# Expert layer's second half: pairs of token tiles prepared per unit, three wide result instructions, more units in pair form

## The chip, the cores and the metric

The kernel runs on one core of one Trainium2 chip. The metric is the device time in microseconds (us) of one execution. The engines are TensorE (PE, matrix products; PEld is its weight load), VectorE (DVE), ScalarE (ACT), GpSimd (POOL) and SyncE (SP, which issues the DMAs).

## The reference, cut to what matters

Three layers follow one another: an attention over 32 pooled memory slots, a layer `g = h * cos(h)` between two products, and a layer of four experts. The change lies in the expert layer:

```python
def _moe2_ref(x, domain_probs, w1, w2):        # x 2304x512, w1 4x512x1024, w2 4x1024x512
    p = domain_probs / (domain_probs.sum(-1, keepdims=True) + 1e-09)
    for e in range(E):
        h = np.maximum(x @ w1[e], 0.0)
        out += p[:, e:e + 1] * (h @ w2[e])
```

All products are carried at about float32 precision: a value is split into a high and a low float32r part, and each product is three matmuls (high by high, high by low, low by high; `mm3`, L340 to L349).

## The kernel before, in words

**Tiling.** The expert layer is cut into 64 units `(u, s, j)`: `u` is one of two halves of the tokens (1152 each), `s` one of 16 slices of 256 hidden features, `j` one of two groups of tokens in a half: 512 tokens (`j=0`, four tiles of 128) and 640 tokens (`j=1`, five tiles).

**First product of a unit** (`hidden`, L1233): `x @ w1` for one slice, as a 2x2 block product in Strassen-Winograd form, with seven block products instead of eight. Each has two chunks of the inner dimension and three matmuls, so a unit is 42 matmuls of 256 or 320 columns. Sums of block products are grown in a PSUM bank, with copies of intermediate states taken by ACT (`a1`, `a2`, `a3`) and sums by DVE (`c11`, `c22`, `c12`). `rectify` (L1296) applies the maximum with zero.

**Second product** (`h @ w2`, added into `acc` with the weight `p`) has two forms. In the *whole* form (`plain_out`, L1384) a tile of 128 tokens takes two feature chunks by three matmuls of 512 columns, and one DVE instruction of 512 elements takes the result out (`gather`, L1098). In the *pair* form (`pair_prep`, L1446 on, `pair_out`, L1525 on) two tiles form a 2x2 block product with seven block products of three matmuls of 256 columns. It needs sums of blocks of `h` beforehand (`sm`), split in high and low (DVE or POOL, and ACT), and prepared sums of blocks of `w2` (`wt`). Its results are taken out between the products: before the change in five instructions of 256 elements and one of 512 per pair, and in the second half of the tokens one of the five runs on ACT into a buffer `ev`, and DVE or POOL adds that to `acc` (`grown`, `plus`).

**Which unit has which form** (`mode`): in `u=0`, slices 2 to 4 are pairs in both groups, slices 5 to 12 in `j=0` alone, all else is whole: 14 of 32 units are pairs. In `u=1` all are pairs but the last. The fifth tile of a `j=1` pair unit goes in the whole form alone (`one_prep`).

**What is around it.** `build_x` makes the seven split operands of the tokens for a group: (0,1) and, at the turn between the halves, (1,0) and (1,1), on ACT, DVE and POOL, with the buffers `sA` and `sB`. `make_wa`, `make_wb` split the weights of slices 7 to 15 during `u=0`; they are stored, and fetched again for `u=1`.

**The order of the work** is fixed when the program is built: `Order` (L167 on) holds tasks that yield operations, estimates when each could start, and issues the earliest, or an older-ranked one within a patience (`PATIENCE`, `RK`). Two settings keep TensorE's operands early: `SLACK` adds a margin in ns to the estimated readiness of an operation of TensorE, by stretch of the work, and `STALL` adds 160 ns where a result would be there less than 60 ns ahead. Buffers are rings (`RINGS`), taken in turn. PSUM has eight banks: four in a ring `p`, four in a ring `po`. The plan of the layers before (`PLAN`) is written out by hand and holds up to about 375 us.

Of the kernel before, what the change touches and what calls it, by code (L numbers as in the profile page):

```python
# [9 lines left out]
F32 = mybir.dt.float32  # L10
# [55 lines left out]
class Have:  # L66
    def __init__(self, keys):
# [73 lines left out]
             p2=2, raw2=2, tt=1, wa=2, wb=2, wt=2, cq=2, p1=2, u2=2, u3=1, ht0=1, ht1=1, h7=4, h7a=2, h7f=3, h1a=1, sma=2, h1=1, sm=2, p=4, po=4, ev=4, eva=2)  # L141
HALVES = (0,)
MERGED = ()
PATIENCE = ({"PE": 0.2, "ACT": 0.5, "DVE": 0.5, "POOL": 0.5, "SP": 0.5, "X": 0.0},
# [3 lines left out]
RK = ((0, -2, 8, 13, 20), (0, -2, 8, 12, 8), (0, -2, 3, 13, 8), (0, -2, 8, 13, 20))  # L148
EV, ONE_P = ((), (0,)), True
RX = (8, 305, 337)  # L150
LAST_PAIR, BP0, WR = 13, 1.5, (-12, 0)
BW, BP, BX, RL = (20.0, 1.5), 1.5, (0.8, 0.8), -15
HOP = 90.0
STALL, SLACK = 160.0, ({"PE": 200.0}, {"PE": 200.0}, {"PE": 300.0}, {"PE": 200.0})
TURNS = (3, 9, 31)
AHEAD = (2, 3, 4, 5, 6)
FULL = (2, 3, 4)
THROUGH = (3, 31)
# [120 lines left out]
def tile_kernel(  # L279
# [13 lines left out]
    nc = tc.nc  # L293
# [511 lines left out]

    def w1_steps(raw, tt, wa):
# [19 lines left out]
    def ready(s):  # L826
# [35 lines left out]
        for f in mixes_of(tt, q[:, 0, 0], q[:, 0, 1], q[:, 1, 0], q[:, 1, 1]):  # L862
            o = yield Op("POOL", 745, lambda: f(nc.gpsimd), t1, port=("POOL",))
# [21 lines left out]
    def ahead(s):  # L885
# [35 lines left out]
        for f in mixes_of(tt, q[:, 0, 0], q[:, 0, 1], q[:, 1, 0], q[:, 1, 1]):  # L921
            o4 = yield either(416, 740, f, o, t1, free=20.0)
# [147 lines left out]
    def mode(i):  # L1070

        u, s, j = units[i]
        if u:
            return "one" if i == FINAL else "pair"
        return "pair" if s in FULL or not j and FULL[-1] < s < LAST_PAIR else "whole"

    def tiles_of(i):

        n = 2 * SUBS[units[i][2]][1] // 128
        if mode(i) == "pair":  # L1080
            return ((n - 2, n - 1), (0, 1)), list(range(2, n - 2))
        return (), list(range(n))

# [66 lines left out]
    def make_wb(s):  # L1150
# [18 lines left out]
        for f in mixes_of(tt, q[:, 0, 0], q[:, 0, 1], q[:, 1, 0], q[:, 1, 1]):  # L1169
            o4 = yield either(416, 740, f, o, t1, free=BW[s > TURNS[0] // 2])  # L1170
# [37 lines left out]
    def build_x(u, j):  # L1208
        if u:
            yield have(*((f"O{i}.{k}e", e) for i, (u_, s, _) in enumerate(units) if not u_ and s and mode(i) == "pair"  # L1210
                         for k in range(2) for e in EV[0]))
            yield have(*(("h7", i, k) for i, (u_, _, _) in enumerate(units) if not u_ and mode(i) == "pair" for k in range(2)))
# [20 lines left out]
    def hidden(i):  # L1233
# [43 lines left out]
        R[rz].give(kz, c11)  # L1277
        R["p1"].give(k1, c11)
# [11 lines left out]
        mids[i] = c, kc, px, kx, py, ky, u2, k2, a2, o4, c11, c22, last, tc_  # L1290
# [5 lines left out]
    def rectify(i):  # L1296
# [29 lines left out]
        hts[i] = which, kh
        if s > FULL[-1]:
# [386 lines left out]
```

## Time and profile before

| | us |
|---|---|
| time, median of 3 runs (lowest to highest) | 1120.25 (1119.69 to 1120.79) |
| span of the profiled execution, first to last instruction | 1118.8 |
| PE busy / weight load busy | 1109.8 / 1055.6 |
| DVE busy | 879.0 |
| POOL busy | 668.5 |
| ACT busy | 583.7 |

The span is the profiled execution's own time; the median of the timed runs is 1.45 us longer, which is what lies around the span. A product on PE lasts longer than the distance to the next one's start, since products are pipelined: how fast PE works is read from the distance between starts.

### The profile page before, as it was taken

What the parts mean: (1) busy time and instruction counts of PE and PEld (TensorE: products, weight loads), DVE (VectorE), ACT (ScalarE), POOL (GpSimd) and SP (SyncE); (2) the same over time, 40 slices, a digit from 0 to 9 for tenths busy, and PEclk for the clock granted to TensorE, in tenths of its full rate; (3) what the DMA queues carried; (4) which work ended last, traced back from release to release, by engine and by line L of the source; (5) the groups of instructions that cost most, each with busy time, mean ns of one, the idle gap of its engine ahead of it and who ended that gap; (6) DMA issues with size and microseconds to landing.
All of it is one profiled execution on the core that took longest, in us unless ns stands there. A gap on an engine that the chain in (4) does not pass through costs nothing.

```text
span 1118.8 us, 22424 instructions
## 1 busy us (share of the span) xinstructions
PE 1109.8 (99%) x8698; PEld 1055.6 (94%) x8698; DVE 879.0 (79%) x1619; ACT 583.7 (52%) x1219; POOL 668.5 (60%) x1001
## 2 busy tenths in 40 slices
PE   9899999999999999999999999999999999999998
PEld 8689999999999989999999999989999999999997
DVE  5888988898888765777888888778777777777776
ACT  4887766565655424444444543445455545554543
POOL 1455556665677404665767664217587877777774
PEclk9999999999999999999999999999999999999999
DMA  9940636167614037443566456683554345434532
GB/s 305 359 137 25 213 129 228 57 227 266 254 39 180 1 118 250 161 161 114 186 253 237 181 181 232 247 337 130 191 205 174 142 167 214 185 142 154 215 131 86
DMA packets 44299, 201.76 MB, mean 180 GB/s; under 512 B 6176, under 2 KB 15392, under 8 KB 29984
## 3 DMA queue, kind: packets, MB, share of 16 engines
q1 hardware_dynamic: 44192, 200.33, 49.1%
q8 instruction: 68, 1.11, 0.4%
q14 instruction: 39, 0.32, 0.1%
HBM read 132.68 MB, written 67.63 MB: 179 GB/s over the span
## 4 chain that ended last, share of the span: by engine, by line
PE 97%; DMA 1%; DVE 1%; SPq 0%; ACT 0%; issue 0%
PE op L342 52%; PE hp L342 41%; DMA q<-in_qt_dram 1%; PE vw_ps L629 1%; PE warm L765 1%; PE kvp L513 1%; PE spare L757 1%; PE sc L566 0%; SPq L370 0%; PE pe L487 0%; DVE st L576 0%; PE pkt L535 0%; DVE sA L390 0%; ACT u L373 0%; DVE stT L596 0%
## 5 line engine op out<-in xcount | busy, mean ns | idle before, releaser
L342 PE MATMUL hp<-x,wa 128*128 128x320 f32 (+1 forms) x2688 | 405.7, 296 | 0.7 <-ACT u L373 0.5
L1103 DVE SCALAR_TENSOR_TENSOR acc<-op,p_all,acc 128x256 f32<-128x256 f32 (+1 forms) x566 | 301.9, 566 | 121.6 <-PE op L342 117.3
L342 PEld LDWEIGHTS hp<-x,wa 128*128 128x128 f32 x2688 | 373.6, 188 | 5.7 <-ACT u L373 1.2
L342 PE MATMUL op<-gt,wo 128*128 128x288 f32 x1536 | 218.1, 296 | 0.0
L342 PEld LDWEIGHTS op<-gt,wo 128*128 128x128 f32 x1536 | 208.1, 188 | 4.5 <-issue 2.4
L390 POOL TENSOR_TENSOR sm<-c 128x128 f32<-128x128 f32 x180 | 88.2, 496 | 157.6 <-ACT c L373 156.5
L342 PE MATMUL op<-wb,h 128*128 128x256 f32 (+1 forms) x786 | 144.7, 298 | 0.0
L342 PE MATMUL op<-wt,h 128*128 128x256 f32 x888 | 143.3, 281 | 0.0
L373 ACT ACTIVATE u<-hp 128x320 f32<-128x320 f32 (+1 forms) x128 | 52.6, 411 | 154.3 <-PE hp L342 154.3
L342 PEld LDWEIGHTS op<-wt,h 128*128 128x128 f32 x888 | 124.7, 189 | 2.4
L342 PEld LDWEIGHTS op<-wb,h 128*128 128x128 f32 x786 | 116.8, 189 | 3.9
L342 PE MATMUL op<-wb,hg 128*128 128x512 f32 (+1 forms) x477 | 115.5, 385 | 0.0
L342 PE MATMUL hp<-attnT,vw 128*128 128x288 f32 x768 | 113.2, 296 | 0.2 <-DVE attnT L390 0.2
L342 PEld LDWEIGHTS hp<-attnT,vw 128*128 128x128 f32 x768 | 105.2, 188 | 3.5 <-issue 1.6
L390 POOL TENSOR_TENSOR gt<-y,gt 128x576 fp32r<-128x576 f32 x41 | 60.0, 1463 | 79.1 <-ACT gt L373 74.7
L342 PEld LDWEIGHTS op<-wb,hg 128*128 128x128 f32 x477 | 84.8, 188 | 15.5
L736 DVE TENSOR_TENSOR acc<-op,acc 128x576 f32<-128x576 f32 (+1 forms) x120 | 84.7, 710 | 18.6 <-PE op L342 17.3
L390 POOL TENSOR_TENSOR h<-c,h 128x128 fp32r<-128x128 f32 (+1 forms) x140 | 84.3, 621 | 15.8 <-ACT h L373 15.8
L1089 DVE TENSOR_TENSOR c<-hp,u 128x320 f32<-128x320 f32 (+1 forms) x128 | 57.9, 452 | 33.5 <-PE hp L342 24.5
L373 ACT ACTIVATE kk<-hp 128x576 int32<-128x576 f32 x64 | 41.6, 650 | 45.2 <-PE hp L342 45.0
L373 ACT ACTIVATE h<-sm 128x512 fp32r<-128x512 f32 x74 | 46.6, 629 | 34.4 <-POOL sm L390 34.3
L373 ACT ACTIVATE c<-c 128x256 f32<-128x256 f32 (+1 forms) x138 | 55.2, 434 | 14.9 <-DVE c L1089 14.9
(144 smaller groups left out, 1644.8 us busy)
## 6 DMA issues: line engine op xcount, KB each, us to landing
wa<-wa_d SPq DMA_DIRECT2D x21, 1792.0 KB, 8.7
wa_d<-wa SPq DMA_DIRECT2D x16, 1792.0 KB, 10.3
wt<-wt_d SPq DMA_DIRECT2D x21, 1024.0 KB, 4.9
wb<-wb_d SPq DMA_DIRECT2D x21, 1024.0 KB, 7.0
raw<-in_w_dram SPq DMA_DIRECT2D x32, 512.0 KB, 4.9
wt_d<-wt SPq DMA_DIRECT2D x16, 1024.0 KB, 7.3
wb_d<-wb SPq DMA_DIRECT2D x16, 1024.0 KB, 6.7
kv<-in_kv_dram SPq DMA_DIRECT2D x16, 512.0 KB, 7.9
```

The costliest lines, as they stand in the source:

```text
L342: nc.tensor.matmul(out=ps, lhsT=lt(a), rhs=rt(b), start=first and i == 0, stop=last and i == 2, skip_group_check=more,)
L373: return Op("ACT", ns, fn or (lambda: nc.scalar.activation(out=out, in_=in_, func=func, **kw)), *deps, table=table)
L390: eng.tensor_tensor(out=out, in0=in0, in1=in1, op=op)
L513: nc.tensor.matmul(out=kvp[32 * i:32 * i + 32], lhsT=es[:n, c, 32 * i:32 * i + 32], rhs=kv[i // 2][0][0][:, c, i % 2] if c < NC else kv[i ...
L629: nc.tensor.matmul(out=ps[32 * i:32 * i + 32, g, j * FS:j * FS + FS], lhsT=kvT[b][64 * g:64 * g + 64, 1, i, :], rhs=wi[s][0][64 * g:64 * g ...
L736: e = yield dve(155 + 301 * nd, lambda: nc.vector.tensor_tensor(out=dst, in0=op[:, :, :TH], in1=dst, op=ALU.add), o)
L757: nc.tensor.matmul(out=bank, lhsT=ones, rhs=ones, start=True, stop=True, skip_group_check=True)
L765: nc.tensor.matmul(out=warm[:, :128], lhsT=ones, rhs=ones, start=True, stop=True)
L1089: return dve(157 + 1.045 * n, lambda: nc.vector.tensor_tensor(out=out, in0=ps, in1=sb, op=ALU.add), *deps)
L1103: nc.vector.scalar_tensor_tensor(out=dst, in0=ps, scalar=pe, in1=dst, op0=ALU.mult, op1=ALU.add)
```

## The change

It touches the expert layer alone; the plan of the layers before stays. In words:

- `mode`: pair form for all units of `u=0` but seven (`WHOLE`): one of `j=0` in slice 0 and in slice 9, five of `j=1` in slices 8, 10, 12, 14 and 15.
- `hidden`: the state `a1` is copied by ACT into a PSUM bank of its own (ring `z`, one bank), and the block product 2 is added to it there; the DVE sum `c11` is gone.
- `pair_prep`: once per unit for both pairs, with instructions of 512 and 256 elements in place of 256 and 128.
- `pair_out`: two banks side by side (`duo`); after the second product ACT copies one block from PSUM to PSUM, and three DVE instructions of 512 elements take the results out. The path over `ev` is gone.
- Rings: `p` has three banks for the first products and all whole tiles, `z` one, `po` two places of two banks. One ring `ht` of two places, a place being a unit's split `h`, replaces `ht0`, `ht1`, `h7`, `h7a`, `h7f`.
- Second products of `u=1` wait in the order for the last step of `build_x(1, 1)`.
- Three small products (`reach`) touch the new banks once.
- The settings of the order are others: among them `SLACK` is 0 in three of four stretches.

```diff
-             p2=2, raw2=2, ... cq=2, p1=2, u2=2, u3=1, ht0=1, ht1=1, h7=4, h7a=2, h7f=3, h1a=1, sma=2, h1=1, sm=2, p=4, po=4, ev=4, eva=2)
+             p2=2, raw2=2, ... cq=2, u2=1, u3=1, ht=2, h1=1, sm=1, p=3, z=1, po=2)
...
-RX = (8, 305, 337)
+RX = (28, 317, 385)
+WHOLE = ((0, 0, 0), (0, 8, 1), (0, 9, 0), (0, 10, 1), (0, 12, 1), (0, 14, 1), (0, 15, 1))
-STALL, SLACK = 160.0, ({"PE": 200.0}, {"PE": 200.0}, {"PE": 300.0}, {"PE": 200.0})
+STALL = 160.0
+SLACK = ({'PE': 0.0}, {'PE': 0.0}, {'PE': 0.0}, {'PE': 300.0})
...
-        if u:
-            return "one" if i == FINAL else "pair"
-        return "pair" if s in FULL or not j and FULL[-1] < s < LAST_PAIR else "whole"
+        return "one" if i == FINAL else "whole" if units[i] in WHOLE else "pair"
...
     def hidden(i):
-        a1 = yield a_(n, p1, px[:, :n], ACTF.Copy, o1, t1)
-        o2 = yield mm(pz, 2, t0)
+        a1 = yield a_(n, pz, px[:, :n], ACTF.Copy, o1, t0)
         o6 = yield mm(px, 6, a1, more=True)
-        c11 = yield sum_(n, c[:, 0, :n], pz[:, :n], p1, o2, a1, tc_)
+        c11 = yield mm(zs[0], 2, a1, more=True)
...
     def plain_out(i, tt, name, at, key, free):
-        yield have(("x", 0, 1))
+        yield have(("x", u, 1))
...
+    def pair_prep(i, before_, mine):
+        t13 = yield two_(512, s13, cv[:, :, :, 1], first, *deps, free=fr)
+        h1 = yield a_(512, ab[0], cv[:, :, :, 0], ACTF.Copy, go, th)
+        t2 = yield two_(256, s24[:, 0], cv[:, 1, :, 1], s13[:, 0], t13, free=fr)
+        t4 = yield two_(256, s24[:, 1], cv[:, 1, :, 0], s24[:, 0], t2, free=fr)
+        h2 = yield a_(256, b2[0][:, 0], cv[:, 1, :, 1], ACTF.Copy, go, th)
+        h3 = yield a_(512, f13[0], sm[0], ACTF.Copy, t13, th)
+        l1 = yield two_(512, ab[1], cv[:, :, :, 0], f32(ab[0]), h1, free=fr)
+        h4 = yield a_(512, f24[0], sm[1], ACTF.Copy, t4, th)
+        l3 = yield two_(512, f13[1], sm[0], f32(f13[0]), h3, free=fr)
+        l2 = yield two_(256, b2[1][:, 0], cv[:, 1, :, 1], f32(b2[0][:, 0]), h2, free=fr)
+        l4 = yield two_(512, f24[1], sm[1], f32(f24[0]), h4, free=fr)
...
     def pair_out(i, k, name):
-        yield have(("h7", i, k), ("wb", u, s), ("wt", u, s), before_, ("x", 0, 1))
+        yield have(("h7", i), ("wb", u, s), ("wt", u, s), before_, ("x", u, 1))
...
+        duo = ps_q.tile([128, 4 * HD2], F32, tag="q", name="op")
+        pz, px, py = (duo[:, HD2 * c:HD2 * c + HD2] for c in (1, 2, 3))
...
+        m1 = yield prod(px, 0, 0, t0, done["h7", i], done["wb", u, s], done["wt", u, s], start=True)
+        m5 = yield prod(py, 3, 3)
+        z1 = yield a_(HD2, pz, px, ACTF.Copy, m5)
+        m6 = yield prod(px, 5, 4, z1)
+        m2 = yield prod(pz, 1, 1)
+        e1 = yield gather(DM, db, duo[:, 2 * HD2:], pb, first, m6)
+        m7 = yield prod(px, 4, 5, e1)
+        m3 = yield prod(py, 2, 6)
+        e2 = yield gather(DM, turned(db), duo[:, 2 * HD2:].rearrange("p (x d) -> p x d", x=2), pb, False, m3)
+        m4 = yield prod(px, 6, 2, e2)
+        e3 = yield gather(DM, da, duo[:, HD2:3 * HD2], pa, first, m4)
...
```

## Rows read from the trace of the kernel before

**Rows 1.** The page: engines (busy us, share, count), clock slices, the chain's shares.
```profile
PE 1109.8 (99%) x8698; PEld 1055.6 (94%) x8698; DVE 879.0 (79%) x1619; ACT 583.7 (52%) x1219; POOL 668.5 (60%) x1001
...
PEclk9999999999999999999999999999999999999999
...
PE 97%; DMA 1%; DVE 1%; SPq 0%; ACT 0%; issue 0%
```

**Rows 2.** Stretches: from:to, length, busy us per engine (count), clock, DMA.
```profile
350.00:400.00 50.00, 49.41 (x357) 47.91 (x356) 41.01 (x59) 24.67 (x45) 22.70 (x19) 1.00 0.23 83
...
600.00:650.00 50.00, 50.00 (x342) 47.27 (x342) 42.63 (x91) 24.98 (x53) 34.01 (x52) 1.00 0.57 206
...
750.00:800.00 50.00, 49.88 (x366) 48.13 (x365) 40.96 (x80) 26.47 (x69) 31.00 (x57) 1.00 0.48 179
...
850.00:900.00 50.00, 50.00 (x387) 49.45 (x386) 37.10 (x74) 25.14 (x66) 37.17 (x67) 1.00 0.46 169
```

**Rows 3.** Timeline of PE: start us, length us, line, operation, count.
```profile
428.45 1.60 PE L342 MATMUL hp<-x,wa 128*128 128x256 f32 x12
429.88 4.37 PE L342 MATMUL op<-wb,hg 128*128 128x512 f32 x18
434.09 2.80 PE L342 MATMUL hp<-x,wa 128*128 128x320 f32 x18
436.73 0.88 PE L342 MATMUL op<-wb,hg 128*128 128x256 f32 x6
437.44 0.52 PE L342 MATMUL op<-wt,hg 128*128 128x256 f32 x3
```

**Rows 4.** ACT by form.
```profile
L373 ACT ACTIVATE ev<-op,p_all 128x256 f32<-128x256 f32 x56 | 26.1, 466 | 0.9 <-PE op L342 0.9
...
L373 ACT ACTIVATE p<-hp 128x320 f32<-128x320 f32 x32 | 13.7, 430 | 24.5 <-PE hp L342 24.5
L373 ACT ACTIVATE p<-hp 128x256 f32<-128x256 f32 x32 | 11.8, 369 | 4.6 <-PE hp L342 4.6
```

**Rows 5.** DVE by form.
```profile
L1103 DVE SCALAR_TENSOR_TENSOR acc<-op,p_all,acc 128x256 f32<-128x256 f32 x378 | 173.8, 477 | 59.7 <-PE op L342 56.7
L1103 DVE SCALAR_TENSOR_TENSOR acc<-op,p_all,acc 128x512 f32<-128x512 f32 x188 | 140.1, 746 | 61.8 <-PE op L342 60.7
...
L390 DVE TENSOR_TENSOR h<-sm,h 128x256 fp32r<-128x256 f32 x81 | 59.0, 752 | 0.0
...
L1089 DVE TENSOR_TENSOR c<-hp,p 128x320 f32<-128x320 f32 x32 | 15.4, 482 | 5.4 <-PE hp L342 4.7 <-issue 0.3 <-POOL hx L390 0.2
...
L390 DVE TENSOR_TENSOR wa<-raw,wa 128x256 fp32r<-128x256 f32 x27 | 11.0, 453 | 0.0
```

**Rows 6.** POOL by form.
```profile
L390 POOL TENSOR_TENSOR sm<-c 128x128 f32<-128x128 f32 x180 | 88.2, 496 | 157.6 <-ACT c L373 156.5
...
L390 POOL TENSOR_TENSOR h<-sm,h 128x256 fp32r<-128x256 f32 x67 | 49.1, 744 | 0.2
...
L390 POOL TENSOR_TENSOR x<-acc,x 128x512 fp32r<-128x512 f32 x3 | 3.9, 1296 | 6.5 <-ACT x L373 6.5
```

**Rows 7.** The chain that ended last, a stretch of the second half.
```profile
843.89 3.54 PE op L342 x24
...
866.45 3.54 PE op L342 x24
```

**Rows 8.** Timeline at the start and the turn: build steps and PE.
```profile
389.14 0.97 PE L342 MATMUL hp<-x,wa 128*128 128x256 f32 x6 [0.47 <-ACT u L373]
...
394.15 0.82 DVE L390 TENSOR_TENSOR x<-sB,x 128x640 fp32r<-128x640 f32 x1
...
741.19 0.73 ACT L373 ACTIVATE x<-acc 128x640 fp32r<-128x640 f32 x1
...
766.20 0.81 DVE L390 TENSOR_TENSOR x<-sB,x 128x640 fp32r<-128x640 f32 x1
...
767.07 2.81 PE L342 MATMUL hp<-x,wa 128*128 128x320 f32 x18
```

More of the change, by code (lines that the diff above doesn't have):

```diff
@@ L1209, in build_x @@
         if u:
-            yield have(*((f"O{i}.{k}e", e) for i, (u_, s, _) in enumerate(units) if not u_ and s and mode(i) == "pair"
-                         for k in range(2) for e in EV[0]))
-            yield have(*(("h7", i, k) for i, (u_, _, _) in enumerate(units) if not u_ and mode(i) == "pair" for k in range(2)))
+            yield have(*(("h7", i) for i, (u_, _, _) in enumerate(units) if not u_ and mode(i) == "pair"))
         keys = [("H", units.index((u - 1, NS2 - 1, j)))] if u else []
@@ L1452, in pair_prep @@
         c, kc = cs_[i]
-        rs, rh = (R["sm"], R["h7"]) if u else (R["sma"], R["h7f" if s in FULL else "h7a"])
-        ks, ts = yield rs
-        kh, th = yield rh
-        if not u and s not in FULL and kh < 2:
-            yield have(("last", full[2 * kh - 4]))
-            th = done["last", full[2 * kh - 4]]
-        if not u and s in FULL and kh == len(full) - 1:
-            yield have(("last", full[-3]))
-            th = done["last", full[-3]]
-        if u and kh % 4 > 1:
-            yield have("swap")
@@ new lines, in pair_prep, with parts @@
+        if u:
+            sm = wc.tile([128, 2, 512], F32, tag="tt", name="sm", bufs=1)
+            sm = [sm[:, k] for k in range(2)]
+        else:
+            sm = [tx.tile([128, 512], F32, tag=tag, name="sm") for tag in ("sA", "sB")]
+        ht = slot().rearrange("p (x o t) -> p x o t", x=2, o=7)
+        go = done["c", i]
+        cv = c[:, :, :512].rearrange("p f (k x t) -> p f k x t", k=2, x=2)
+        def parts(o, n=1):
+            return [ht[:, x, o:o + n].rearrange("p o (k t) -> p o k t", k=2) for x in range(2)]
@@ new lines, in flat @@
+        def flat(o, n):
+            return [ht[:, x, o:o + n].rearrange("p o t -> p (o t)") for x in range(2)]
+        s13 = sm[0].rearrange("p (o k t) -> p o k t", o=2, k=2)
+        s24 = sm[1].rearrange("p (o k t) -> p o k t", o=2, k=2)
+        first = cv[:, 0].rearrange("p k x t -> p x k t")
+        deps = (go, ts, done["wt", 0, NS2 - 1] if u else None)
+        t13 = yield two_(512, s13, cv[:, :, :, 1], first, *deps, free=fr)
+        ab, b2 = parts(0, 2), parts(2)
+        h1 = yield a_(512, ab[0], cv[:, :, :, 0], ACTF.Copy, go, th)
@@ L1572, in pair_out, with reach @@
-        e6 = None
-        if not first:
-            e6 = yield gather(HD2, db[:, 1], py, pb, False, m5, m2)
-        m7 = yield prod(px, 5, 5, e3, more=True)
-        e5 = yield from grown(2, db[:, 1], px, pb, m7)
-        if first:
-            e6 = yield gather(HD2, db[:, 1], py, pb, False, m5, m2)
-        m4 = yield prod(px, 2, 6, e5, more=True)
-        m3 = yield prod(py, 6, 2, e6, more=True)
-        (R["h7"] if u else R["h7f" if s in FULL else "h7a"]).give(kh, m3)
-        used(u, s, "wb", R["wb"], kb_, m3)
+        if len(duos) < 2:
+            duos.append(None)
+            def reach():
+                nc.tensor.matmul(out=pz, lhsT=ht[:, 0, 0, :128], rhs=b[0](0), start=True, stop=True)
+            t0 = yield pe(120, 130, reach, t0, done["h7", i], done["wb", u, s])
@@ L1644, in tile_kernel, with free @@
                     continue
[L1646 removed]
+                def free(o, i=i, t=t, n_=len(rest)):
                     _, ring, k1 = ones_[i, t]
[L1648 removed]
+                    todo.count((ring, "one", i), 1 if ring == "h1" else n_, R[ring], k1, o)
                 def at(tt, i=i):
[L1651 removed]
+                    return lambda x, fc: ones_[i, tt][0][:, x, fc]
                 todo.add(f"Q{i}.{g}", 10 * i + RK[phase(i)][2] + g, one_prep(i, t, *prep_turn(i, t + 9)))
                 todo.add(f"O{i}.{g}", 10 * i + RK[phase(i)][3] + g, plain_out(i, t, f"O{i}.{g}", at, ("h1", i, t), free))
[L1655 to L1661 removed]
         todo.run()
```

289 lines of the change are left out of this document (92 added, 197 removed), and 3 rows, old and new, of the table PATIENCE.

## The prediction

> **What bounds the kernel now.** I read the page first. PE is busy for 99% of the span and holds 97% of the chain that ended last, at the full granted clock of 2.4 GHz in every slice [rows 1]. A busy PE need not be a fast PE, so the table of stretches and the timeline come next. In the expert layer PE is busy for 50.00 of 50 us in nearly all stretches; what is visibly idle is 0.59 us at the layer's start and 0.12 us at the turn between the halves, 0.7 us in all [rows 2]. The timeline gives the distance from start to start. 12 products of 256 columns take 429.88 - 428.45 = 1.43 us, 119.2 ns each; 18 of 512 take 4.21 us, 233.9 ns each; 18 of 320 take 2.64 us, 146.7 ns each; six of 256 in a pair's second product take 0.71 us, 118.3 ns each [rows 3]. They follow each other without holes, so the layer's time is the number of products times these distances, and everything else is cover. DVE (74 to 85%) and POOL (68 to 74%) are loaded, but neither holds the chain [rows 1, 2].
>
> **The change part by part.**
>
> *More pairs (the main term).* Before, 14 units of the first half are pairs, each with two pairs: 28. After, 32 - 7 = 25 units: 50. The second half has 31 pair units in both. So 22 pairs of tiles change form. Two tiles in the whole form are 12 products of 512 columns: 12 x 233.9 = 2.81 us. As a pair they are 7 x 3 = 21 of 256: 2.48 us at 118.3 ns, 2.50 us at 119.2 ns [rows 3]. A pair saves 0.30 to 0.32 us; 22 save 6.7 to 7.1 us, and I take 6.9. This is on the path, since PE has no holes to swallow it. The first product keeps its 42 matmuls per unit in all 64 units.
>
> The Trainium skill, "TensorE: Matmul & The Clock Gate", section "Back-to-back issue gap", speaks against this term: it gives a sustained 81 ns per matmul at 128 columns and 131 ns at 512. By a straight line between them 256 columns would cost 98 ns, 21 of them 2.05 us against 1.57 us for 12 wide ones, and the change would lose about 10.6 us (an estimate from that page). The rows show 233.9 ns at 512 columns, not 131, so the measured distances decide, and the rule gets no share of the chance.
>
> *The three `reach` products.* One of 320 columns and two of 256 by the distances above: 0.15 + 2 x 0.12 = 0.4 us on PE.
>
> *Outlet of a pair.* Before, five instructions of 0.477 us and one of 0.746 us, in the second half one of the five on ACT (0.466 us) with an addition elsewhere [rows 4, 5]. After, three of 0.746 us on DVE and one ACT copy. DVE per pair falls from 5 x 0.477 + 0.746 = 3.13 us (2.65 us with `ev`) to 2.24 us. It is off the path, and so worth nothing by itself. What counts is the chain: the products wait in turn for the copy z1, for e1 and for e2. With about 0.3 us for the two hand-overs of each wait (my estimate) that is 0.37 + 0.75 + 0.75 + 0.9 = 2.8 us, of which the pair's own m2 covers 0.36: 2.4 us to be covered by other work. Before, three waits of 0.48 + 0.3 us with two products beside them left 1.6 us. There is cover: in the second half a slice of four pairs takes 866.45 - 843.89 = 22.56 us [rows 7], 5.64 us a pair, of which 2.49 us are the pair's own; 3.15 us of first products and single tiles remain, and a second open pair besides. So I cost the longer chain at nothing. If the cover went, it would be up to 2.4 us for each of 112 pairs.
>
> *First product.* The sum c11 (0.482 us at 320 columns [rows 5], 64 times) leaves DVE; product 2 now waits for a1, as product 6 did before. ACT's copy goes to PSUM. The trace has no such copy; the nearest rows are those from PSUM to the other memory, 0.369 and 0.430 us [rows 4]. Product 5 (six matmuls, 0.71 or 0.88 us) lies beside it. If the copy were 0.1 us shorter or longer, nothing on PE would move; I take zero. At twice the time (0.74 or 0.86 us) with 0.3 us of hand-overs, 0.3 us in each of 64 units would be bare if nothing else stood in the queue: 19 us, the far end of this unknown, and the rows are far from it.
>
> *Preparation per unit.* The same 2816 elements in 7 two-input instructions instead of 16, and on ACT 1792 in 4 instead of 6. On POOL a unit costs 4 x 1.30 + 3 x 0.74 = 7.4 us where two pairs cost 2 x (4 x 0.50 + 0.5 + 3 x 0.74) = 9.4 us [rows 6]. In `u=1` POOL and DVE both become lighter. In `u=0` with the weights of slices 7 to 15, a slice with two pair units gains one more preparation (7.4 us on POOL, or about 4 us on DVE) but sheds two outlets' surplus (1.8 us), two sums (0.9 us) and the whole unit's own splitting on DVE; slices with a whole unit only shed. From 85% on DVE and 68% on POOL [rows 2] I see no engine that fills up, and take zero.
>
> *Margins and PSUM.* `SLACK` falls from 200 or 300 ns to 0 in three of four stretches, so results are planned to land nearer to their use; three banks in `p` in place of four make one unit's first product wait for the one before it to be rectified. Lower bound: the 0.7 us of idle time vanish (-0.7 us). Upper bound: of about 112 x 3 + 64 x 4 = 590 waits a tenth is late by 60 ns, the distance that `STALL` looks at: +3.6 us. Nearest row: the idle time now, 0.7 us [rows 2]. I take it once more: +0.7 us.
>
> *The rest* (the other formula for `wt`, with as many operations; the layers before, whose plan stays) is zero.
>
> Sum: -6.9 + 0.4 + 0.7 = -5.8 us against the profiled execution (span 1118.8 us and 1.45 us around it). From the median of 1120.25 us that gives **1114.5 us**. Its own range is 1112.8 us (idle time gone, 7.1 us saved) to 1117 us (margins at +3.2 us).
>
> **The rivals.**
>
> *A. The builds at the start and at the turn lose their cover.* At the turn (1,1) is built from 741.19 to 767.0 us, 25.8 us, and PE goes on at 767.07, just as it ends [rows 8]. Second products of `u=1` now queue behind its last step. What PE then has: two first products of 256 columns (2 x 42 x 0.119 = 10.0 us) and ten whole tiles (14.0 us), of which two (2.8 us) were gone by that time before: 21.2 us. Short by 4.6 us, if the build is as slow. Against it: its longest queue is 11 instructions of some 0.82 us on DVE, 9 us, so it can be done earlier; here only the rank and the cover decide. At the start unit 1 now needs (0,1) and a preparation before its second product, where its four whole tiles stood before; that build ended at 395.0 us [rows 8], and two first products, four whole tiles and the rest of the layer before take PE to about 395 us. Price there: 0 to 2 us. With 4.6 us for both the time is 1113.8 + 4.6 = **1118.4 us**.
>
> *B. Slower: wide preparations hold up the outlets.* DVE's preparation of 256 elements takes 0.752 us on average where instructions of this width that stand alone more often take 0.453 us [rows 5]: POOL and DVE hinder each other. POOL's step grows from 0.74 to 1.30 us [rows 6], so a gather queued behind such a DVE instruction comes up to 0.56 us later than before, in a chain whose need for cover has grown from 1.6 to 2.4 us. With one bare hit in every second pair unit, 28 x 0.56 = 15.7 us: 1113.8 + 15.7 = **1129.5 us**. It makes the kernel slower from (6.5 + 2.2) / 0.56 = 16 bare hits on. For it: `SLACK` is gone. Against it: PE has no hole now at 85% on DVE, and DVE and POOL lose work.
>
> The Trainium skill, "SBUF — State Buffer", section "Who interferes with whom", states that a DVE instruction with two inputs in SBUF contends with a GpSimd instruction that reads SBUF, under an exclusive lock; the longer mean above agrees. By that rule a full wait would be POOL's whole 1.30 us.
>
> *C. The change does less than it says*, because the two forms differ less where they stand between others: at two thirds of 6.7 us, 4.5 us come off, and with 0.4 and 0.7 us added the time is **1116.9 us**. The rows in both forms speak against it.
>
> **How the numbers follow.** Forecast 0.65, A 0.18, B 0.11, C 0.06. A measurement here can tell 0.2%, 2.2 us: faster is below 1118.0, slower above 1122.5. The forecast and C are faster. A is faster where the shortfall stays under 4.2 us (0.08 of its 0.18), else the same (0.10). B ends slower with 0.08, the same with 0.02, faster with 0.01. Faster 0.80, same 0.12, slower 0.08. The range that leaves out two in ten reaches from 1111.8 us, just beyond the forecast's lower end, to 1118.5 us, past A's value.
>
> **What would show it.** Right: in the changed trace 2352 products of 256 columns and 384 of 512 in the second products (1890 and 648 now), at unchanged distances; stretches of the second half at 50.00 of 50 us; fewer DVE and POOL us there; the turn without more than 2 us idle. Idle PE at about 385 to 396 us or at the turn, released by ACT or DVE's x, shows A. Many small waits for `acc<-op` on DVE through the layer show B. A 512-column product spaced closer than 230 ns, or a 256-column one wider than 122 ns, makes the main term wrong.

## The result and the profile after

The changed kernel takes **1132.64 us** (median of 5 runs, the fastest 1130.55) against 1120.25 us: a ratio of **1.0111** (95% interval 1.008 to 1.0143). One of the five runs, of 3798.86 us, was a slow one and is left out of the ratio. It is slower by 12.4 us, where 5.8 us less were forecast. That is rival B's side, 3 us beyond its price.

The page of the kernel after (engines, clock slices, chain), to be held against [rows 1]:

```profile
PE 1117.3 (98%) x8899; PEld 1066.1 (94%) x8899; DVE 894.1 (79%) x1439; ACT 609.9 (54%) x1248; POOL 507.6 (45%) x518
...
PEclk9899999999999899999999999999999999999999
...
PE 35%; DVE 2%; ACT 0%; issue 0%; ACTq 0%
```

The shares hardly move, and POOL is much lighter (508 us against 668). Two things tell. The shares of the chain sum to 37% where they summed to 99: followed back from the end it gets no further than 717 us, where it leaves PE for a weight's split on DVE. And there are two clock slices below 9. The first is peculiar to this execution (its span is 1136.6 us, 1138.49 us timed; from 40 to 50 us, in the first layers, the granted clock is 0.53, which costs it about 5 us); the second stands behind a hole that the change opened, see below.

The stretches of the kernel after, columns as in [rows 2]:

```profile
350.00:400.00 50.00, 47.40 (x338) 46.90 (x338) 37.03 (x51) 24.60 (x43) 28.71 (x25) 0.93 0.19 80
...
550.00:600.00 50.00, 48.32 (x356) 46.00 (x355) 46.67 (x77) 26.22 (x58) 28.68 (x34) 1.00 0.42 155
...
700.00:750.00 50.00, 47.59 (x355) 45.79 (x354) 45.49 (x75) 26.91 (x60) 24.58 (x26) 1.00 0.52 192
750.00:800.00 50.00, 48.64 (x325) 45.16 (x324) 37.32 (x57) 24.94 (x56) 18.83 (x16) 1.00 0.66 260
...
850.00:900.00 50.00, 50.00 (x389) 49.37 (x389) 35.04 (x57) 25.20 (x63) 15.95 (x14) 1.00 0.52 196
```

Before, PE was busy for 49.41, 49.88 and 50.00 us in the first, fourth and last of these stretches [rows 2]. Now there is idle PE from 500 to 800 us, in which the later slices of the first half run and the weights of slices 7 to 15 are split (the first step on POOL at 509 us), and DVE (46.67 and 45.49 us) is at 91 to 93% in its worst stretches. The second half, all pairs as before, has next to none, and DVE is lighter there (35.04 against 37.10 us), as forecast.

**Counting the holes.** A product's busy time covers part of a hole, since products overlap. I therefore sum, over all neighbouring products, the distance from start to start beyond the usual 118.5, 147 and 233.5 ns (256, 320 and 512 columns; 133.6 ns for 288), where it is longer by over 12 ns:

| us of holes | 375–410 | 410–500 | 500–590 | 590–740 | 740–800 | 800– | all | pairs in the first half | median less before's |
|---|---|---|---|---|---|---|---|---|---|
| before | 1.1 | 0.3 | 0.0 | 0.1 | 0.4 | 0.1 | 2.0 | 28 | |
| after | 6.1 | 0.5 | 5.3 | 7.6 | 2.4 | 1.1 | 23.0 | 50 | +12.4 |
| e1_z_bank | 3.0 | 0.8 | 5.0 | 7.6 | 2.4 | 1.1 | 19.9 | 50 | +10.4 |
| e2_light_pool | 3.9 | 0.8 | 1.8 | 4.3 | 2.3 | 1.0 | 14.1 | 50 | +6.0 |
| e3_light_both | 5.2 | 0.8 | 2.4 | 4.3 | 2.2 | 1.0 | 15.9 | 50 | +5.9 |
| e4_slack | 6.5 | 1.2 | 2.7 | 14.4 | 4.6 | 11.2 | 40.6 | 50 | +31.1 |
| e5_no_splits | 5.1 | 0.9 | 1.5 | 3.6 | 3.1 | 1.3 | 15.5 | 58 | +1.8 |
| e6_old_form_more | 1.1 | 0.0 | 3.2 | 6.6 | 3.8 | 0.1 | 14.8 | 38 | +9.2 |
| e7_one_pair_unit | 3.0 | 2.3 | 2.7 | 2.6 | 2.6 | 9.2 | 22.4 | 44 | +15.4 |
| e8_same_units | 3.0 | 0.8 | 4.4 | 6.8 | 2.3 | 1.1 | 18.4 | 50 | +9.0 |
| e9_one_unit_margin | 2.7 | 0.0 | 3.9 | 1.5 | 1.8 | 2.0 | 11.9 | 44 | +3.8 |
| e10_one_unit_margin_b | 3.0 | 0.9 | 3.8 | 2.7 | 2.2 | 1.0 | 13.6 | 44 | +5.8 |

For each row "holes less before's 2.0, less 0.31 us for every pair more, plus 0.4 for the small products" gives the last column within 3 us, mostly a little above it: after 21.0 - 6.8 + 0.4 = 14.6 for 12.4; e7 20.4 - 5.0 + 0.4 = 15.8 for 15.4; e9 9.9 - 5.0 + 0.4 = 5.3 for 3.8; e6, without the small products, 12.8 - 3.1 = 9.7 for 9.2. So every run fits with the forecast gain per pair, to within those 3 us, and what has to be explained is the holes.

**Where DVE's time went.** The stretch 500 to 800 us of the kernel before, then of the kernel after:

```profile
500.00:800.00 300.00, 299.88 (x1993) 280.78 (x1993) 245.92 (x489) 139.44 (x303) 170.55 (x262) 1.00 0.55 207
```

```profile
500.00:800.00 300.00, 292.20 (x2067) 276.50 (x2066) 259.81 (x426) 158.37 (x346) 152.34 (x165) 1.00 0.53 201
```

DVE gains 13.9 us, POOL loses 18.2. The groups of DVE's preparations in that stretch, before and after (count, then busy us and mean ns):

```profile
L390 DVE TENSOR_TENSOR h<-sm,h 128x256 fp32r<-128x256 f32 x24 | 15.8, 694 | 0.0
...
L390 DVE TENSOR_TENSOR h<-c,h 128x256 fp32r<-128x256 f32 x12 | 8.2, 684 | 0.0
...
L390 DVE TENSOR_TENSOR hx<-sm,hx 128x256 fp32r<-128x256 f32 x14 | 6.6, 508 | 0.0
```

```profile
L390 DVE TENSOR_TENSOR ht<-sm,ht 128x512 fp32r<-128x512 f32 x28 | 28.4, 1013 | 0.0
...
L390 DVE TENSOR_TENSOR ht<-c,ht 128x256 fp32r<-128x256 f32 (+1 forms) x25 | 19.1, 765 | 0.0
L390 DVE TENSOR_TENSOR sm<-c,sm 128x256 f32<-128x256 f32 x21 | 14.6, 695 | 1.2 <-POOL sm L390 0.7
L390 DVE TENSOR_TENSOR sm<-c 128x512 f32<-128x512 f32 x15 | 10.3, 684 | 2.0 <-ACT c L373 2.0
...
```

Preparation on DVE grew from 30.6 to 72.4 us (73.7 with a small group not shown). By the same view the weights' splits and sums (`wa`, `wb`, `wt`, `tt`) came over from POOL too: 37.0 to 49.2 us. What I had counted as shed was shed: outlets 122.4 to 113.0, sums of the first product 35.0 to 22.1, whole units' splits 28.1 to 13.2, builds 12.9 to 8.6 us. 43.1 + 12.2 - 9.4 - 12.9 - 14.9 - 4.3 = 13.8 us, near the 13.9 of the two rows (the groups overlap a little, so each kernel's groups add up to more than its row).

**How a hole comes about.** Waits of PE's weight loads in the same stretch (us in total, times, longest), then one case on the timeline (DVE, POOL and PE; in brackets the idle time before, and what ended it):

```profile
PEld op L342 <- DVE acc L1107: 9.7, 18, 1.2
PEld hp L342 <- ACT u L373: 3.0, 5, 0.9
```

```profile
738.18 1.81 DVE L390 TENSOR_TENSOR ht<-sm,ht 128x512 fp32r<-128x512 f32 x1
739.91 1.40 DVE L1107 SCALAR_TENSOR_TENSOR acc<-op,p_all,acc 128x512 f32<-128x512 f32 x2
...
738.15 1.29 POOL L390 TENSOR_TENSOR x<-acc,x 128x512 fp32r<-128x512 f32 x1
...
738.76 1.04 PE L342 MATMUL z<-x,wa 128*128 128x320 f32 x6
740.70 0.98 PE L342 MATMUL op<-wt,ht 128*128 128x256 f32 x6 [0.89 <-DVE acc L1107]
```

POOL starts 0.03 us ahead of a DVE split of 512 elements, which then takes 1.81 us where one of this width takes 0.68 undisturbed (the `sm<-c` row above). The gather behind it starts at 739.91, and PE, out of other work, stands for 0.89 us. The Trainium skill, "SBUF — State Buffer", section "Who interferes with whom", says that a two-input DVE instruction contends with GpSimd's reads for a port locked by one of them. The row agrees: the extra 1.13 us is nearly POOL's whole 1.29.

The case is typical in one respect. In this stretch PE itself stood 12 times for a gather, 5.1 us in all, and each time DVE went on to that gather without a pause from the instruction ahead of it: in ten cases a preparation or a weight's split, with POOL running beside it in seven, and in two another gather.

**The start and the turn.** PE's hole in the kernel after at the start, DVE and ACT beside it, and the stretches behind the hole:

```profile
391.30 1.01 PE L342 MATMUL hp<-x,wa 128*128 128x256 f32 x3 [2.60 <-ACT u L373]
...
388.76 0.82 DVE L390 TENSOR_TENSOR sB<-sA,acc 128x640 f32<-128x640 f32 x1
...
389.62 0.74 ACT L373 ACTIVATE x<-sB 128x640 fp32r<-128x640 f32 x1 [1.95 <-DVE sB L390]
390.26 0.72 ACT L373 ACTIVATE x<-sA 128x640 fp32r<-128x640 f32 x1
390.89 0.36 ACT L373 ACTIVATE u<-hp 128x256 f32<-128x256 f32 x1
```

```profile
390.00:395.00 5.00, 3.70 (x17) 3.70 (x18) 3.38 (x7) 3.19 (x8) 1.56 (x1) 0.57 0.00 0
395.00:400.00 5.00, 5.00 (x29) 4.73 (x29) 3.13 (x6) 2.66 (x6) 0.00 (x0) 0.75 0.00 0
```

The copy `u`, which PE needs, stands on ACT behind two steps of the build of (0,1), and these wait for DVE: rival A's place, at 2.6 us. Behind the hole the granted clock is 0.57 and 0.75, that is the level of 1.2 GHz for part of ten microseconds. That does not follow every time: the run e2 below has the same order and the same hole, and its clock stayed at 1.00. Its PE, and the stretch behind the hole:

```profile
390.89 3.60 PE L342 MATMUL hp<-x,wa 128*128 128x256 f32 x24 [2.60 <-ACT u L373]
...
390.00:395.00 5.00, 4.05 (x30) 3.74 (x30) 4.01 (x8) 3.48 (x9) 1.56 (x1) 1.00 0.00 0
```

At the turn, PE waits for ACT again. ACT ahead of the first and of the second of these waits, and one more such wait on PE far from the turn, stand behind:

```profile
766.68 0.98 PE L342 MATMUL hp<-x,wa 128*128 128x256 f32 x6 [0.36 <-ACT u L373]
768.20 1.70 PE L342 MATMUL hp<-x,wa 128*128 128x256 f32 x12 [0.53 <-ACT u L373]
...
779.59 1.58 PE L342 MATMUL hp<-x,wa 128*128 128x256 f32 x11 [0.47 <-ACT u L373]
...
765.64 0.72 ACT L373 ACTIVATE x<-sA 128x640 fp32r<-128x640 f32 x1
...
767.76 0.38 ACT L373 ACTIVATE u<-hp 128x256 f32<-128x256 f32 x1 [1.13 <-PE hp L342]
...
611.88 2.02 PE L342 MATMUL hp<-x,wa 128*128 128x320 f32 x12 [0.59 <-ACT u L373]
```

That is 1.4 us, not the 4.6 that A priced. In the first of the three (0.36 us) the copy `u` follows a step of the build on ACT, which is A's place. In the other two ACT had itself just waited for PE (1.13 us at 767.76, 1.07 us ahead of the third), and so it had at 611.88: here the first product's own chain of products, copies and sums shows, with no other product between. In the kernel before, PE has no such wait from 500 to 800 us; now it has 2.0 us of them.

### The profile page after: what moved, and what is told of

It reads as the page before. It is cut to its first block, busy times and chain, and to the rows that moved or that the text cites. A ratio compares the mean times of both kernels' runs of the same rounds, so it can differ in the third digit from the quotient of the medians.

```text
span 1136.6 us, 22254 instructions
## 1 busy us (share of the span) xinstructions
PE 1117.3 (98%) x8899; PEld 1066.1 (94%) x8899; DVE 894.1 (79%) x1439; ACT 609.9 (54%) x1248; POOL 507.6 (45%) x518
## 5 line engine op out<-in xcount | busy, mean ns | idle before, releaser
L342 PE MATMUL hp<-x,wa 128*128 128x320 f32 (+1 forms) x2304 | 358.0, 298 | 4.9 <-ACT u L373 4.6
L342 PEld LDWEIGHTS hp<-x,wa 128*128 128x128 f32 x2304 | 322.9, 190 | 9.3 <-ACT u L373 5.8
L1107 DVE SCALAR_TENSOR_TENSOR acc<-op,p_all,acc 128x512 f32<-128x512 f32 x382 | 277.9, 746 | 66.0 <-PE op L342 63.7
L342 PE MATMUL op<-wb,ht 128*128 128x256 f32 (+1 forms) x1236 | 226.4, 303 | 3.2 <-DVE acc L1107 3.0
L342 PE MATMUL op<-wt,ht 128*128 128x256 f32 x1344 | 206.3, 281 | 2.7 <-DVE acc L1107 1.9
L342 PEld LDWEIGHTS op<-wb,ht 128*128 128x128 f32 x1236 | 184.3, 188 | 16.1 <-DVE acc L1107 5.7
L342 PEld LDWEIGHTS op<-wt,ht 128*128 128x128 f32 x1344 | 181.2, 188 | 5.3 <-DVE acc L1107 4.7
L373 ACT ACTIVATE ht<-sm 128x512 fp32r<-128x512 f32 x112 | 67.1, 625 | 20.9 <-POOL sm L390 13.3
L390 POOL TENSOR_TENSOR ht<-sm,ht 128x512 fp32r<-128x512 f32 x41 | 60.3, 1471 | 16.2 <-ACT ht L373 12.0
L390 DVE TENSOR_TENSOR ht<-sm,ht 128x512 fp32r<-128x512 f32 x71 | 65.9, 928 | 1.8 <-ACT ht L373 1.8
```

The costliest lines, as they stand in the source:

```text
L342: nc.tensor.matmul(out=ps, lhsT=lt(a), rhs=rt(b), start=first and i == 0, stop=last and i == 2, skip_group_check=more,)
L373: return Op("ACT", ns, fn or (lambda: nc.scalar.activation(out=out, in_=in_, func=func, **kw)), *deps, table=table)
L390: eng.tensor_tensor(out=out, in0=in0, in1=in1, op=op)
L1107: nc.vector.scalar_tensor_tensor(out=dst, in0=ps, scalar=pe, in1=dst, op0=ALU.mult, op1=ALU.add)
```

## The experiments

In each, the kernel before ran on the same chip, and the table above has the holes.

**e1_z_bank: the order at the start.** The bank pairs are allocated ahead of the bank `z`, so that the small products come behind the last products of the layer before, whose results the build of (0,1) takes; in the kernel after, pieces of the expert layer's first products run ahead of these.

```diff
-    ps_z = ctx.enter_context(tc.tile_pool(name="ps_z", bufs=1, space=PSUM, reuse_waits="tile"))
     ps_q = ctx.enter_context(tc.tile_pool(name="ps_q", bufs=2, space=PSUM, reuse_waits="tile"))
+    ps_z = ctx.enter_context(tc.tile_pool(name="ps_z", bufs=1, space=PSUM, reuse_waits="tile"))
```

> The changed kernel with the bank of the ring z taken from the other end of PSUM (the pool opened after that of the ring po): the order of every engine is that of the changed kernel, but the second step of the first unit can no longer slip in between the last products of the layers before. Theory (start): these 18 early products push the last products of the layers before 2.2 us back, the build of (0,1) with them, and ACT's copy a3 stands behind it; so the 2.6 us hole at 388 us goes and the stretch at half clock behind it too; from 380 to 405 us PE stands idle under 1.5 us, time 3 to 5 us lower, 1128 to 1129.5 us. Rival (three banks in p make the start slow): hole and time stay within 1 us.

Measured: 1130.17 us, ratio to before 1.0093 (1.0076 to 1.011). PE at the start:

```profile
381.43 0.41 PE L1274 MATMUL z<-x,wa 128*128 128x320 f32 x1 [0.85 <-DVE acc L736]
...
385.43 3.62 PE L342 MATMUL hp<-x,wa 128*128 128x256 f32 x24 [0.64 <-ACT u L373]
```

Holes of 0.85 and 0.64 us stand in place of 2.6, and the clock stays at 1.00. PE is idle for 1.6 us from 380 to 405 us, where under 1.5 was expected, and the time is 0.7 us above the expected range. The loss to the kernel before falls from 12.4 to 10.4 us; the two intervals overlap, and the execution of the kernel after whose mean clock was 1.000 took 1130.55 us, about as long as e1, so most of these 2 us can be the clock behind the hole. The 15 us in 500 to 800 stay.

**e2_light_pool and e3_light_both: the weights' load.** POOL (in e3 DVE as well) writes zeros in place of the low parts of the weights of slices 7 to 15, so those parts are left out of the products; the order of the instructions is the same.

```diff
+        if LITE[0] and any(eng is x for x in (nc.gpsimd,)):
+            eng.memset(f32(out), 0.0)
+            return
```

> The changed kernel, in the same order of work; where POOL would compute a low part of the weights of slices 7 to 15, it writes zeros instead (the low parts are left out of the result), so POOL reads nothing there. Theory B (POOL's reads stretch DVE's wide splits, and the outlets queued behind them come late): PE's holes from 500 to 800 us, 15.6 us now, fall to 10 us or less, DVE's ht<-sm of 512 elements from 928 to under 850 ns, time about 1127 us. Rival (the outlet's longer chain with two places and three banks, whatever DVE does): holes 14 us or more, time 1131 to 1134 us.

> As the run before, and DVE too writes zeros where it would compute a low part of these weights (left out of the result). Theory B with load: DVE from 500 to 750 us falls below 85% busy, holes to 5 us or less, time about 1122 us. Rival (chain): holes 12 us or more, time above 1129 us.

Measured: e2 1125.75 us, 1.0061 (1.0044 to 1.0078); e3 1125.68 us, 1.0056 (1.0041 to 1.0071). The stretch 500 to 800 of e2, its DVE group answering to the one above and the waits of its weight loads there, and the same stretch of e3:

```profile
500.00:800.00 300.00, 296.06 (x2115) 282.40 (x2114) 251.09 (x433) 162.43 (x356) 116.88 (x166) 1.00 0.54 201
```

```profile
L395 DVE TENSOR_TENSOR ht<-sm,ht 128x512 fp32r<-128x512 f32 x29 | 25.5, 879 | 0.0
...
PEld op L342 <- DVE acc L1119: 4.0, 10, 0.9
PEld hp L342 <- ACT u L373: 2.8, 4, 0.8
```

```profile
500.00:800.00 300.00, 295.62 (x2114) 281.95 (x2114) 245.19 (x433) 163.17 (x357) 117.12 (x165) 1.00 0.54 202
```

Taking POOL's reads away (and 35 us of its time with them), with not one instruction moved, took 6.9 us of the 15.3 us of holes in 500 to 800, 8.7 us off DVE, and the mean of the wide split from 1013 to 879 ns (over the whole run from 928 to 877, where under 850 was expected). POOL was not what PE waited for (the waits above name DVE), nor did DVE wait for POOL's results for more than 0.9 us in this stretch, in either run. So this is POOL's work beside DVE, as rival B had it; whether by its reads or by its mere length (a write of zeros takes 0.31 us, the split 0.83 us and more) this run does not tell apart. The waits for gathers fall from 9.7 to 4.0 us; those for ACT's copy `u` stay (3.0 and 2.8 us), and are part of what is left. e3 missed: 6 us less on DVE again change nothing, though it is as light as before the change (245.19 against 245.92 us). The other 8 to 9 us are not a matter of DVE's sum.

**e4_slack: the margins of before.** Margins of 200, 200, 300 and 200 ns in the four stretches of the order, in place of 0, 0, 0 and 300.

```diff
-SLACK = ({'PE': 0.0}, {'PE': 0.0}, {'PE': 0.0}, {'PE': 300.0})
+SLACK = ({'PE': 200.0}, {'PE': 200.0}, {'PE': 300.0}, {'PE': 200.0})
```

> The changed kernel with the margins of the kernel before (SLACK 200, 200, 300, 200 ns), planned anew. Rival (margins: results land just late because the order left none): holes in the expert layer fall to 8 us or less, time 1118 to 1123 us. Theory B: margins only reorder; the cover is short anyway, holes stay at 15 us or more, time 1130 us or more.

Measured: 1150.88 us, 1.0281 (1.0265 to 1.0296). Its stretches:

```profile
500.00:800.00 300.00, 287.42 (x2019) 271.56 (x2018) 256.04 (x429) 158.15 (x342) 136.88 (x150) 0.99 0.51 193
800.00:1100.00 300.00, 296.72 (x2241) 288.15 (x2240) 220.03 (x333) 137.53 (x348) 96.60 (x80) 1.00 0.44 174
```

That the missing margins make the holes is refuted, for the margins of before. Two things happen: with the larger margins there are more holes in 500 to 800 (21.7 us for 15.3), and with the *smaller* one at the end, 200 for 300, the second half has 11.2 us of holes where it had 1.1.

**e5_no_splits: pairs without the weights.** Slices 7 to 15 fetch the stored weights of slices 2 to 6 (so the products there are of other weights) and split none; three units stay whole.

```diff
-WHOLE = ((0, 0, 0), (0, 8, 1), (0, 9, 0), (0, 10, 1), (0, 12, 1), (0, 14, 1), (0, 15, 1))
+WHOLE = ((0, 0, 0), (0, 14, 1), (0, 15, 1))
+        for s in range(7, NS2):
+            saved[s] = saved[2 + s % 5]
...
-            if s in AHEAD:
+            if s > 1:
```

> Slices 7 to 15 take in the first half the stored split weights of slices 2 to 6 (fetched by DMA, so the sums there are of other weights) and split none of their own; whole units are three, (0,0,0), (0,14,1) and (0,15,1), so four more units are pairs. Theory (the pair form fails where a slice's weights are split beside it: in the 31 pair units of the second half and in slices 0 to 6, where nothing is split, TensorE has no holes): the holes in 500 to 800 fall from 15.6 us to 4 to 6, of them under 2 in 500 to 700, the rest at the turn; with eight more pairs at 0.3 us less each the time is 1132.6 - 10.5 - 2.4 = 1119 to 1122. Rival (the outlet and the preparation of a pair by themselves leave holes whenever a unit of the first half is a pair): as with DVE's and POOL's own splits made light, holes of 8 to 9 us in 500 to 800, and 1124 to 1126. Rival (the fetches come late instead): holes behind DMAs, 1130 or more.

Measured: 1122.5 us, 1.0019 (1.0009 to 1.0028). The stretch 500 to 800:

```profile
500.00:800.00 300.00, 297.81 (x2213) 287.07 (x2212) 239.04 (x371) 143.39 (x348) 56.74 (x51) 1.00 0.45 174
```

Just beyond the expected time (1119 to 1122), although nearly every unit is a pair. But the holes are 8.2 us in 500 to 800 where 4 to 6 were expected (the first rival's 8 to 9), and 3.2 in 500 to 700 where under 2 were. So about half of the holes go with the splitting and half stay without it.

**e6_old_form_more: the old form with more pairs.**

```diff
-LAST_PAIR, BP0, WR = 13, 1.5, (-12, 0)
+LAST_PAIR, BP0, WR = 16, 1.5, (-12, 0)
-FULL = (2, 3, 4)
+FULL = (2, 3, 4, 5, 6)
```

> The kernel before with five more pair units in its own form (both groups of slices 5 and 6, one group of slices 13 to 15; 19 in place of 14 of the first half's 32 units), nothing else changed. Theory (what costs is the number of pair units in slices whose weights are split beside them, in either form; the wide form eases it rather than causes it): holes of 15 to 25 us in 500 to 800, time 1130 to 1142, more lost per added unit than after's 11. Rival (the wide instructions of 512 elements make the holes, and the form with instructions of 256 has none): ten more pairs at 0.3 us less each, 1116 to 1118.

Measured: 1129.93 us, 1.0088 (1.0073 to 1.0103), where the rival said 1116 to 1118. The stretch 500 to 800 of this run, and PE in its worst place:

```profile
500.00:800.00 300.00, 293.26 (x2002) 276.05 (x2001) 241.57 (x488) 145.26 (x327) 217.80 (x343) 0.99 0.54 199
...
714.91 0.62 PE L342 MATMUL op<-wt,hx 128*128 128x256 f32 x3 [0.89 <-DVE acc L1103]
716.51 0.80 PE L342 MATMUL op<-wt,hx 128*128 128x256 f32 x2 [0.99 <-DVE acc L1103]
```

The old form loses too, gathers of 256 elements now standing behind splits of 256: 10 more pairs open 13.1 us of holes in 500 to 800 (13.6 less 0.5), 1.3 us a pair, or 2.2 if only the 6 that lie in slices 7 to 15 are counted. (Some 1.7 us of the 13.1 are products at the lower clock, 0.66 from 715 to 720 us.) The wide form opened 14.8 us for 22, 0.7 a pair, or 1.2 for each of the 12 in slices 7 to 15. A pair gains 0.31. So the width by itself is not to blame: in either form the pairs that were added beside the splits opened holes of several times what they bring. DVE is even lighter here than before the change (241.57 against 245.92 us); it is POOL that gained (217.80 against 170.55). The settings of the order are those chosen for the units of before; what better ones would have closed is not known. (Theory's 15 to 25 us of holes and 1130 us were a little too much.)

**e7_one_pair_unit and e8_same_units.** In slices 7 to 15 only the group of 512 tokens is a pair; both runs have e1's bank order, and settings of the order chosen anew, each for itself: patience and the weighting of DVE against POOL, in e7 also ranks and the margins below. e8 has after's own units and after's own margins.

```diff
-WHOLE = ((0, 0, 0), (0, 8, 1), (0, 9, 0), (0, 10, 1), (0, 12, 1), (0, 14, 1), (0, 15, 1))
+WHOLE = ((0, 0, 0), (0, 7, 1), (0, 8, 1), (0, 9, 1), (0, 10, 1), (0, 11, 1), (0, 12, 1), (0, 13, 1), (0, 14, 1), (0, 15, 1))
...
-SLACK = ({'PE': 0.0}, {'PE': 0.0}, {'PE': 0.0}, {'PE': 300.0})
+SLACK = ({'PE': 40.0}, {'PE': 40.0}, {'PE': 120.0}, {'PE': 200.0})
```

> The changed kernel with the new bank order at the start, and other units in pair form: slices 0 to 6 all but one unit, and of slices 7 to 15 (whose weights are split beside them) only the group of 512 tokens: 22 pair units in the first half, 6 fewer pairs than after and 16 more than before. The order's settings are chosen anew for this set. Theory (two pair units in a slice with splits are what DVE and POOL cannot carry in time; one per slice they can, as the kernel before does): holes in 500 to 800 of 1 to 4 us against 15.6; against before 16 pairs less 0.31 us each (-5.0), the start +1.9, the holes +0.3 to +3.3: 1117 to 1120.5, a little faster than before. Rival (each wide pair beside the splits costs its 0.7 us wherever it stands: 18 such pairs here, 24 in after): holes of 11 to 12 us, 1127 to 1129.

> Control for the last run: the new bank order at the start and the order's settings chosen anew in the same way, with after's own pair units kept. Theory (the units matter, not the settings): holes in 500 to 800 of 12 to 16 us, 1127 to 1130.5, as with the bank order alone. Rival (it was the settings): holes under 6 us, 1121 or less.

Measured: e7 1135.83 us, 1.0133 (1.0111 to 1.0155), a clear miss; e8 1129.48 us, 1.0076 (1.0054 to 1.0098), as expected of a control. The stretch 590 to 740 of e8, then of e7, and what e7's weight loads waited for behind 800 us:

```profile
590.00:740.00 150.00, 146.53 (x1017) 137.96 (x1016) 133.73 (x234) 82.08 (x176) 76.32 (x86) 1.00 0.57 218
```

```profile
590.00:740.00 150.00, 149.30 (x1008) 139.95 (x1008) 120.92 (x222) 76.64 (x158) 66.93 (x79) 1.00 0.58 222
```

```profile
PEld op L342 <- DVE acc L1107: 6.1, 24, 0.3
```

In the middle the theory held: from 590 to 740 DVE goes from 133.73 to 120.92 us and the holes from 6.8 to 2.6. The two runs differ in settings as well as in units, but three sets of settings with after's units (7.6 us with its own, 14.4 in e4, 6.8 in e8) stand against three with these (2.6 here, 1.5 and 2.7 below). In 500 to 800 in all, 7.9 us are left, more than the 1 to 4 expected and less than the rival's 11 to 12. And the second half, which I had taken as given, lost 9.2 us: it was planned with a margin of 200 ns (and some other settings), the value at which e4 has 11.2 us of holes there.

**e9_one_unit_margin and e10_one_unit_margin_b.** The same units and bank order as e7, the second half's settings back to the changed kernel's (300 ns), two different sets for the first half. Of the settings the diff shows e9's margins, against those of e7; in e10 they are 40, 200, 120 and 300 ns.

```diff
-SLACK = ({'PE': 40.0}, {'PE': 40.0}, {'PE': 120.0}, {'PE': 200.0})
+SLACK = ({'PE': 80.0}, {'PE': 120.0}, {'PE': 80.0}, {'PE': 300.0})
```

> The last set of units again (in slices 7 to 15 only the group of 512 tokens as a pair), with the order's settings of the second half as the changed kernel has them (margin 300 ns in place of 200), and those of the first half chosen anew. Theory (the 9.4 us lost behind 800 us in the last-but-one run are its smaller margin there, and one pair unit per slice with splits is bearable): holes behind 800 us back under 1 us, 550 to 700 under 2 us, 500 to 800 in all 3 to 6 us; start 3 us, 410 to 500 under 1 us: against before 16 pairs less 0.31 us (-5.0), +1.9 at the start, +3 to +6 in 500 to 800: 1120 to 1123.5. Rival (the holes wander: where one stretch is mended another opens, as long as DVE's outlets of the pairs stand behind wide preparations): 15 us of holes or more in all, 1127 or more.

> The same units and the same settings of the second half, with other settings of the order in the first half, to see how far these alone move the time. Theory: as the run before it, 1120 to 1124; rival (the settings of the first half decide): more than 3 us from it.

Measured: e9 1123.99 us, 1.0032 (1.002 to 1.0044); e10 1126.02 us, 1.0052 (1.0038 to 1.0065). e9's stretch 590 to 740:

```profile
590.00:740.00 150.00, 149.51 (x1016) 140.90 (x1014) 128.72 (x234) 76.24 (x158) 60.81 (x69) 1.00 0.59 223
```

e9 stands 0.5 us above its expected range, e10 2 us; e9's holes are 7.2 us in 500 to 800 where 3 to 6 were expected. The second half has 2.0 and 1.0 us of holes in place of 9.2 (under 1 was expected), and 590 to 740 again 1.5 and 2.7. The settings of the first half alone are worth 2 us, the distance of the two runs. The comparison with before that frames it: e9 loses 3.8 us to it where the changed kernel loses 12.4, with six pairs fewer. What neither mends is 500 to 590 us, where the splitting of weights sets in beside slices that are pairs throughout: 3.9 and 3.8 us, and 2.7 to 5.3 in every experiment that splits there in full. That stretch stays open. No version here beats the kernel before.

## Why the prediction was wrong

- **More pairs, -6.9 us: right.** Products by their columns: 2354 of 256, two of them the small ones, and 384 of 512, as forecast. The distance of the kernel after, from 861.24 to 862.65 us for twelve products of 256 columns, is 117.5 ns:

```profile
861.24 0.52 PE L342 MATMUL op<-wb,ht 128*128 128x256 f32 x3
...
862.65 0.61 PE L342 MATMUL hp<-x,wa 128*128 128x320 f32 x3
```

- **First product, zero: right for the copy, not for the chain.** The copy from PSUM to PSUM that I had to bound takes 0.366 and 0.423 us, as long as the copies that I went by. But from 500 to 800 us PE waits 2.0 us for ACT's copy `u` where before it had no such wait, 1.6 us of it with no build ahead of `u`. Which part of the change makes that chain late (three banks in `p`, one place for `u`, the step through `z`) no run separates. The copy's rows:

```profile
L373 ACT ACTIVATE z<-hp 128x320 f32<-128x320 f32 x32 | 13.5, 423 | 2.9 <-PE hp L342 2.9
L373 ACT ACTIVATE z<-hp 128x256 f32<-128x256 f32 x32 | 11.7, 366 | 14.3 <-PE hp L342 14.3
```

- **Preparation per unit, zero: this is the step that failed.** I wrote "From 85% on DVE and 68% on POOL [rows 2] I see no engine that fills up, and take zero", with 7.4 us a unit on POOL or about 4 on DVE. In its place the runs show 15.3 us of holes in 500 to 800 us, where before there were 0.5. The order gave most of the preparation to DVE (+43.1 us in that stretch, and 12.2 us of the weights' work with it), to 91 and 93% in its fullest parts, while POOL emptied; the wide split, on DVE beside POOL, took 1013 ns in the mean where 684 is the undisturbed time, and the gathers stood behind such instructions. With POOL's part of the weights made light and nothing else moved, 6.9 us of the holes go (e2). A full DVE is not by itself the price: with DVE as light as before the change e3 still has 8.9 us of holes there, and e6, lighter still, 13.6. I had seen the longer splits in [rows 5] and priced them in rival B, but kept them out of the sum. Which engine gets a step also hangs on settings of the order that came with the change; no run changes these alone.
- **Outlet of a pair, "I cost the longer chain at nothing": wrong with it.** The cover was worked out from [rows 7], a slice of the second half, where no weights are split, and holds there. In 500 to 800 it did not: gathers that started late were bare on PE. What part of the holes is the chain alone is left open: 8 to 9 us of all holes stay when the weights' splits are light or gone (e2, e3, e5), some 2 us of them in e2 by ACT's `u`. Nor did any run give the second product more room (places in `ht` or `po`, banks in `p`), so that rival stands untested.
- **Margins, +0.7 us: wrong mechanism.** Restoring them costs 18 us more (e4); what the smaller ones cost by themselves no run shows. Only the second half's margin works in the way meant: at 200 ns the wide gathers there leave 9 to 11 us of holes (e4, and e7 with other settings besides), and the change raised it to 300.
- **Rival A: half right.** 5 us of holes at the start in after, with the clock, of which 3 came with the order of the first products (e1). The turn costs 1.4 us of waits, 0.4 behind the build and 1.0 by the first product's chain.
- **Rival B: what happened in large part.** 15.3 us of holes in 500 to 800 against its 15.7 is closer than the mechanism: they are 68 gaps of 0.22 us in the mean rather than 28 of 0.56, 6.9 us of them go with POOL's part of the weights, and some 2 us are no gathers at all, so that the near hit in size is partly luck. Its chance of 0.11 was too low. What I set against it, that DVE and POOL lose work, came true for POOL alone: DVE gained 15.1 us in all (879.0 to 894.1 us), 13.9 of them in the stretch that decides. ("POOL (68 to 74%)" was a misreading besides: 62% at 750 to 800 us in [rows 2]; nothing hangs on it.)

## What to carry to other kernels

Price a change in the stretch where the engines are fullest, and ask which engine will be given the work that can go to either. Its share there is a warning, not a price (e3 and e6 have DVE's share of before, and the holes): look at what will stand directly ahead of the instruction that the bounding engine waits for, and how long that takes beside the other engines. Check cover in the stretch where the step is used, not in the one that shows it most cleanly. A saving of 0.31 us on the bounding engine was less here than the 0.7 us of holes that came with it, so try the change first where its side work is free.

## What the hardware showed that I had not expected

A hole of 2.6 us on PE was followed by granted clocks of 0.57 and 0.75 over ten microseconds, so it cost more than its length. But the same hole, of 2.60 us and in the same place, left the clock at 1.00 in e2 and e4 and took it to 0.76 and 0.89 in e3 and 0.66 in e5, so one execution does not price it; behind holes of 0.85 and 0.64 us, some 4 us apart, it stayed at 1.00 (e1). A split of 512 elements on DVE took up to 1.81 us, 2.6 times its undisturbed 0.68. And, of the order rather than of the chip: the margin with which PE's operands are planned works in both directions. With 100 ns less the second half has 9 to 11 us of holes (e4; e7, with other settings too), with 200 to 300 ns more the stretch from 500 to 800 us has another 6.4 (e4).
